# Low halves of ten weight slices: from VectorE to GpSimd

## The chip, the core and the metric

The kernel runs on one core of a Trainium2 chip. The metric is the device time of one execution in microseconds (us). Engines have short names here as in the profile: PE is TensorE (PEld its weight loads), DVE is VectorE, ACT is ScalarE, POOL is GpSimd, SP is SyncE, which issues most DMAs.

## What is computed

Three layers follow one another. The first is gated linear attention over 4 batches and 8 heads, 768 steps of 48 values: a state that decays by `alpha`, takes up `k` times `v`, and is read by `q`. Its output, 3072 tokens of 384 values, goes through a mixture of four experts, and that through a feed-forward layer with a clipped gate:

```
state = alpha[:, :, t, :, None] * state + einsum('bhd,bhe->bhde', k[:, :, t], v[:, :, t])
y[:, :, t] = einsum('bhd,bhde->bhe', q[:, :, t], state)
...
h = np.maximum(x @ w1[e], 0.0); out += p[:, e:e + 1] * (h @ w2[e])      # e = 0..3, 1024 hidden values each
...
h = x @ w_in; g = h * np.clip(h + 3.0, 0.0, 6.0) / 6.0; return g @ w_out   # 2048 hidden values
```

## The kernel before

**Three products for one.** Every matmul of the two layers runs on operands that are rounded to a shorter format. To keep the precision, a weight or an activation is split into a high half (rounded copy) and a low half (what the rounding lost), and three products are summed: high times high, low times high, high times low. A weight slice is 256 hidden values wide; its first matrix (y = 0) and its second (y = 1) each fill a tile of 128 partitions by 768 columns. So "slice i" has four tiles: `w0h`, `w0l`, `w1h`, `w1l`.

**Two phases.** In the first phase, the first some 490 us, the attention is computed, and between its steps PE works on the first seven weight slices (0 to 6: four of expert 0, three of expert 1) for the blocks of tokens as they become ready. The seven slices are split once, at the phase's start, and stay. The rest of the experts and the last layer are the second phase.

**The order is written out.** In the first phase a table of tokens (`PLAN`, then `BLOCK` for each later pair of blocks) sets the order in which the instructions of PE, DVE, ACT and SP are issued; each engine takes its own in order. Some tokens: `m0.6` is the first product of step 6 of visit 0 (line 923, `ph`), where steps 6 and 7 use slice 3; `o0.6` its second product (line 969, `po`); `a0.6` the high half of the result on ACT (line 933, `hh`); `h0.6` its low half on DVE (line 937, `hl`), which also sets the PSUM tile `ph` free for a step further on (two such tiles take turns). Visit 0 is expert 0 (slices 0 to 3), visit 1 expert 1 (slices 4 to 6: `m1.0` to `m1.5`). `r03` and `r13` round the weights of slice 3 on ACT (line 875, first and second matrix), and `l03` and `l13` compute their low halves (line 877). A token of the form `1.Uq3` is a step of the attention: `U` scales `kt` or `qt` in place (line 513), `M` masks the products `pa` (line 538), `S` copies on ACT (line 504).

**Rooms.** The raw weights lie in a few rooms (`rw`, `early_h`, `early_l`). When the low half of a slice is done, its room takes the next raw slice: `room_left` issues that load on SP (lines 859 and 864), which waits for the low half, and everything behind it on SP waits too.

**GpSimd** has no work between its constants at the start and the first weight combinations for the second phase.

The function that the change touches, as it stands before:

Of the kernel before, what the change touches and what calls it, by code (L numbers as in the profile page):

```python
# [11 lines left out]
F32 = mybir.dt.float32  # L12
# [708 lines left out]
def tile_gla__then__moe__then__moe2(  # L721
# [29 lines left out]
    nc = tc.nc  # L751
# [12 lines left out]
    mul, add, sub = ALU.mult, ALU.add, ALU.subtract  # L764
# [104 lines left out]
    def split_w(y, i):  # L869
        round_w(y, i)()  # L870

    def round_w(y, i):
        raw = raws.pop((y, i))
        hi, lo = (wpa.tile([P, 3 * SL], F32R, tag=f"w{y}{z}", name=f"w{y}{z}_{i}") for z in "hl")
        nc.scalar.copy(hi, raw)
        wts[(y, i)] = [t.rearrange("p (j f) -> p j f", j=KT if y == 0 else 2) for t in (hi, lo)]
        return lambda: nc.vector.tensor_tensor(lo, raw, hi.bitcast(F32), op=sub)


    xs = {}  # L880
# [158 lines left out]
    def do(tok, b):  # L1039
# [18 lines left out]
        elif kind == "g":  # L1058
            load_p(int(arg))
        elif kind in "Wrl":  # L1060
            y, i = int(arg[0]), int(arg[1])
            if kind == "W":
                if (y, i) == (1, 3):
                    again(0)
                load_w(y, i)
            elif kind == "r":
                splits[(y, i)] = round_w(y, i)
            else:
                splits.pop((y, i))()
                if (y, i) != (0, 1):  # L1070
                    room_left(y, i)
        else:
            vi, f = (int(x) for x in arg.split("."))
            vi += 2 * b
            if kind == "m":
                splits[(vi, f)] = mm1(vi, f)
            elif kind == "a":
                plan.pop((vi, f))()
            elif kind == "h":
                splits.pop((vi, f))()  # L1080
            elif kind == "o":
                mm2(vi, f)
                if f == len(visits[vi]["steps"]) - 1:
                    after(3, lambda v_=vi + 2: load_p(v_))
            else:
                finish(vi, f)
# [793 lines left out]
    for G in range(NG):  # L1880
        add_group(G)
        i = I_[G]
# [42 lines left out]
```

## Time and profile before

| | us |
|---|---|
| median of three runs | 1330.15 (1329.89 to 1330.52) |
| profiled execution, its own time | 1329.23 |
| its span, first to last instruction | 1327.5 |
| PE busy | 1305.6 (98%) |
| DVE busy | 893.3 (67%) |
| ACT busy | 586.4 (44%) |
| POOL busy | 130.4 (10%) |

The shares are means over stages that differ. DVE is busy for 67% of the span, but in the stage in which the ten low halves lie it is another matter, so the stage has to be read by itself. PE's clock has two levels here, 2.4 GHz (printed as 1.00) and 1.2 GHz (0.50); a number between is a stretch with both.

### The profile page before, as it was taken

What the parts mean: (1) busy time and instruction counts of PE and PEld (TensorE: products, weight loads), DVE (VectorE), ACT (ScalarE), POOL (GpSimd) and SP (SyncE); (2) the same over time, 40 slices, a digit from 0 to 9 for tenths busy, and PEclk for the clock granted to TensorE, in tenths of its full rate; (3) what the DMA queues carried; (4) which work ended last, traced back from release to release, by engine and by line L of the source; (5) the groups of instructions that cost most, each with busy time, mean ns of one, the idle gap of its engine ahead of it and who ended that gap; (6) DMA issues with size and microseconds to landing.
All of it is one profiled execution on the core that took longest, in us unless ns stands there. A gap on an engine that the chain in (4) does not pass through costs nothing.

```text
span 1327.5 us, 26799 instructions
## 1 busy us (share of the span) xinstructions
PE 1305.6 (98%) x10877; PEld 1088.3 (82%) x10877; DVE 893.3 (67%) x1635; ACT 586.4 (44%) x1065; POOL 130.4 (10%) x184
## 2 busy tenths in 40 slices
PE   8899999999999999999999999999999999999998
PEld 7799887888888888888888887888888888888886
DVE  8899977777875354778575557655887674445444
ACT  4655454444454232454442243234556554444442
POOL 4000000000000010323131102021321000000000
PEclk8899999999999999999999999999999999999999
DMA  7765536526342344899999969897965674436323
GB/s 207 208 170 132 163 108 167 148 72 186 108 128 70 116 143 158 252 307 308 352 273 298 253 205 281 250 287 229 265 196 204 233 210 148 148 137 175 127 87 48
DMA packets 164779, 250.75 MB, mean 189 GB/s; under 512 B 73520, under 2 KB 122544, under 8 KB 158128
## 3 DMA queue, kind: packets, MB, share of 16 engines
q1 hardware_dynamic: 145696, 222.90, 51.3%
q0 software_dynamic: 12480, 25.17, 11.4%
q10 hardware_dynamic: 6480, 0.98, 0.5%
q8 instruction: 85, 1.39, 0.4%
q14 instruction: 38, 0.31, 0.1%
HBM read 162.97 MB, written 90.75 MB: 191 GB/s over the span
## 4 chain that ended last, share of the span: by engine, by line
PE 88%; DVE 3%; ACT 3%; issue 2%; DMA 2%; POOL 1%; SPq 0%; ACTq 0%; DVEq 0%; POOLq 0%
PE sum L1637 29%; PE chain_b L1550 15%; PE ph L923 13%; PE chain_a L1550 12%; PE po L969 10%; PE po L1825 2%; PE py L628 2%; PE pa L525 2%; PE py L650 1%; PE pu L573 1%; DMA acc_d<-o 1%; DMA w_d<-da 1%; PE py L611 1%; ACT qt L481 1%; DVE kt L513 1%
## 5 line engine op out<-in xcount | busy, mean ns | idle before, releaser
L1637 PE MATMUL sum<-hh,V 128*128 128x512 f32 x1224 | 376.8, 389 | 0.4 <-DVE o L1687 0.4
L1637 PEld LDWEIGHTS sum<-hh,V 128*128 128x128 f32 x1224 | 229.7, 188 | 48.5 <-DVE o L1687 0.8
L1637 PE MATMUL sum<-hl,V 128*128 128x512 f32 x612 | 238.1, 389 | 0.0
L1570 DVE TENSOR_TENSOR cs<-ct,chain_b 128x512 f32<-128x512 f32 x153 | 105.0, 686 | 148.3 <-PE chain_b L1550 147.0
L1562 ACT COPY ct<-chain_a 128x512 f32<-128x512 f32 x153 | 89.2, 583 | 137.7 <-PE chain_a L1550 137.5
L1637 PEld LDWEIGHTS sum<-hl,V 128*128 128x128 f32 x612 | 114.9, 188 | 23.9
L933 ACT ACTIVATE hh<-ph 128x512 fp32r<-128x512 f32 (+1 forms) x98 | 52.4, 537 | 177.0 <-PE ph L923 175.7
L1587 ACT ACTIVATE hh<-cs 128x512 fp32r<-128x512 f32 x81 | 51.3, 633 | 137.9 <-DVE cs L1570 88.6
L937 DVE SCALAR_TENSOR_TENSOR hl<-ph,hh 128x512 fp32r<-128x512 f32 (+1 forms) x98 | 59.8, 612 | 71.4 <-ACT hh L933 71.3
L1596 ACT ACTIVATE g<-cs,three 128x512 f32<-128x512 f32 x72 | 52.2, 725 | 106.1 <-DVE cs L1570 104.2
L969 PE MATMUL po<-hh,w1h 128*128 128x512 f32 (+1 forms) x249 | 90.7, 372 | 0.0
L969 PE MATMUL po<-hh,w1l 128*128 128x512 f32 (+1 forms) x249 | 86.8, 356 | 0.0
L1601 DVE SCALAR_TENSOR_TENSOR hl<-g,hh 128x512 fp32r<-128x512 f32 x96 | 67.5, 705 | 27.2 <-ACT hh L1598 27.0
L969 PE MATMUL po<-hl,w1h 128*128 128x512 f32 (+1 forms) x249 | 80.7, 355 | 3.2 <-DVE hl L937 3.2
L923 PE MATMUL ph<-xh,w0h 128*128 128x512 f32 (+1 forms) x294 | 77.9, 374 | 2.0 <-DVE hl L937 1.1
L1597 DVE SCALAR_TENSOR_TENSOR g<-g,cs 128x512 f32<-128x512 f32 x72 | 50.4, 701 | 39.2 <-ACT g L1596 39.1
L1590 DVE SCALAR_TENSOR_TENSOR hl<-cs,hh 128x512 fp32r<-128x512 f32 x81 | 57.4, 710 | 28.7 <-ACT hh L1587 28.4
L923 PE MATMUL ph<-xl,w0h 128*128 128x512 f32 (+1 forms) x294 | 74.7, 363 | 0.0
L923 PE MATMUL ph<-xh,w0l 128*128 128x512 f32 (+1 forms) x294 | 74.6, 363 | 0.0
L1598 ACT ACTIVATE hh<-g 128x512 fp32r<-128x512 f32 x96 | 60.2, 630 | 20.9 <-DVE g L1597 18.8
L1688 POOL DMA_DIRECT2D acc_d<-o x54 | 47.9, 903 | 137.3 <-DVE o L1687 135.5
L923 PEld LDWEIGHTS ph<-xh,w0h 128*128 128x128 f32 x294 | 50.5, 191 | 12.2 <-DVE hl L937 3.1
(313 smaller groups left out, 2532.3 us busy)
## 6 DMA issues: line engine op xcount, KB each, us to landing
V<-ws_d SPq DMA_DIRECT2D x34, 1280.0 KB
V<-ws_d SPq DMA_DIRECT2D x34, 768.0 KB
ws_d<-V SPq DMA_DIRECT2D x17, 1280.0 KB
acc_d<-o POOLq DMA_DIRECT2D x54, 256.0 KB, 9.3
ws_d<-V SPq DMA_DIRECT2D x17, 768.0 KB
vl<-vd SPq DMA_DIRECT2D x96, 96.0 KB
draw<-in_moe_w_in_dram SPq DMA_DIRECT2D x8, 768.0 KB
w_d<-da SPq DMA_DIRECT2D x16, 384.0 KB
```

The lines of the kernel that those rows point to most:

```text
L923: pe.matmul(ph[:, 0:n], w[:, j, fs], x[:, j, cs], start=(o == 0 and j == 0), stop=(o == 2 and j == KT - 1),)
L933: high = lambda: nc.scalar.activation(hh[:, 0:n], ph[:, 0:n], AF.Relu)
L937: nc.vector.scalar_tensor_tensor(hl[:, 0:n], ph[:, 0:n], 0.0, hh[:, 0:n].bitcast(F32), op0=ALU.max, op1=sub)
L969: pe.matmul(accs[vi][m][:, 0:n], w[:, z, ms], h[:, 0:n], **fl)
L1550: pe.matmul(chain[bank], a, b, start=first_ and o == 0, stop=o == 2, skip_group_check=True)
L1562: o = act(512, lambda: nc.scalar.copy(CR.place(k), chain[0]), dep, d)
L1570: o = dve(512, lambda: nc.vector.tensor_tensor(SR.place(k), CR[kc], chain[1], op=add), dep, oc, d)
L1590: lambda: nc.vector.scalar_tensor_tensor(HR[k][1], get(), 0.0, HR[k][0].bitcast(F32), op0=ALU.max, op1=sub),
L1596: a = act(600, lambda: nc.scalar.activation(GR.place(kg), get(), AF.Relu, bias=three), dep, dg, opened)
L1598: hh = act(512, lambda: nc.scalar.activation(HR.place(k)[0], GR[kg], AF.Copy, scale=1.0 / 6.0), b, d)
L1601: lambda: nc.vector.scalar_tensor_tensor(HR[k][1], GR[kg], 1.0 / 6.0, HR[k][0].bitcast(F32), op0=mul, op1=sub),
L1637: pe.matmul(bank[(y, m)][:, ts], a, b[:, ts], start=first_ and x == 0, stop=last_ and x == 2, skip_group_check=True)
```

## The change

The low halves of slices 0 and 1 stay on DVE. Those of slices 2 to 6, ten instructions of 128x768, are issued on GpSimd:

```
         nc.scalar.copy(hi, raw)
         wts[(y, i)] = [t.rearrange("p (j f) -> p j f", j=KT if y == 0 else 2) for t in (hi, lo)]
-        return lambda: nc.vector.tensor_tensor(lo, raw, hi.bitcast(F32), op=sub)
+        low = nc.vector if i < 2 else nc.gpsimd
+        return lambda: low.tensor_tensor(lo, raw, hi.bitcast(F32), op=sub)
```

The order of PE, ACT and SP is the same before and after; DVE has ten rows fewer and POOL ten rows more. From here on, line numbers of the changed kernel are higher by one.

On DVE, at the first two low halves that move (slice 2; `w0l`, `w1l`), the order was this (`w` and `rq`, `dg` and `rq`, `kt` and `qt` are attention steps, `hl` is the low half of a result of step 1 and then of steps 2 and 3):

```order
L937 SCALAR_TENSOR_TENSOR hl_0_762<-ph_1_833,hh_0_761 128x256
L877 TENSOR_TENSOR w0l_846<-early_l,w0h_845 128x768
L877 TENSOR_TENSOR w1l_851<-early_l,w1h_850 128x768
L287 TENSOR_TENSOR w_2_914<-rq_704,rk_705 128x768
L513 TENSOR_TENSOR qt_790<-qt_790,tl_1_809 128x128x4
L345 TENSOR_REDUCE dg_917<-w_2_914 128x16
```

and now it is this; the two low halves are gone and `w` follows `hl` at once:

```order
L938 SCALAR_TENSOR_TENSOR hl_0_762<-ph_1_833,hh_0_761 128x256
L287 TENSOR_TENSOR w_2_914<-rq_704,rk_705 128x768
L513 TENSOR_TENSOR qt_790<-qt_790,tl_1_809 128x128x4
L345 TENSOR_REDUCE dg_917<-w_2_914 128x16
L290 TENSOR_TENSOR rq_704<-rq_704,ra_706 128x768
L513 TENSOR_TENSOR kt_769<-kt_769,tl_1_811 128x64x8
```

On POOL all ten stand behind the last constant (`mask`), in the order of the table, with slice 3's second matrix (`w1l_973`) ahead of its first (`w0l_1032`), and ahead of the first weight combination of the second phase (`spare_l`):

```order
L174 AFFINE_SELECT mask<-mask 64x64 x8
L878 TENSOR_TENSOR w0l_846<-early_l,w0h_845 128x768
L878 TENSOR_TENSOR w1l_851<-early_l,w1h_850 128x768
L878 TENSOR_TENSOR w1l_973<-early_h,w1h_972 128x768
L878 TENSOR_TENSOR w0l_1032<-rw_3_717,w0h_1031 128x768
L878 TENSOR_TENSOR w0l_1066<-early_h,w0h_1065 128x768
L878 TENSOR_TENSOR w1l_1069<-early_l,w1h_1068 128x768
L878 TENSOR_TENSOR w0l_1314<-early_l,w0h_1313 128x768
L878 TENSOR_TENSOR w1l_1498<-early_h,w1h_1497 128x768
L878 TENSOR_TENSOR w0l_1564<-early_h,w0h_1563 128x768
L878 TENSOR_TENSOR w1l_1595<-early_l,w1h_1594 128x768
L1478 TENSOR_TENSOR spare_l<-spare_h 128x256
```

Where DVE had `w1l_973` behind seven attention steps, POOL takes it as soon as its high half is there.

## Rows read from the trace of the kernel before

**Rows 1.** Windows: us, then PE, PEld, DVE, ACT, POOL busy, clock, DMA, GB/s.

```profile
50.00:100.00 50.00, 48.92 (x894) 45.36 (x893) 48.99 (x96) 28.13 (x54) 0.00 (x0) 0.93 0.68 189
```

**Rows 2.** Chain that ended last, 85 to 98 us: start us, length us, what.

```profile
90.77 0.34 DVE hl L937
...
91.16 1.34 PE ph L923 x9
...
97.59 0.34 DVE hl L937
...
97.97 0.39 PE ph L923
```

**Rows 3.** Waits of PE, 92 to 490 us: total us, times, longest.

```profile
PE ph L923 <- DVE hl L937: 0.7, 2, 0.3
```

**Rows 4.** Timeline of DVE, slice 2's low halves: start us, length us, instruction.

```profile
50.28 0.95 DVE L877 TENSOR_TENSOR w0l<-early_l,w0h 128x768 fp32r<-128x768 f32 x1
51.15 0.95 DVE L877 TENSOR_TENSOR w1l<-early_l,w1h 128x768 fp32r<-128x768 f32 x1
```

**Rows 5.** Timeline of POOL and DVE, where DVE reads PSUM (`po`).

```profile
465.42 0.46 POOL L1478 TENSOR_TENSOR spare_l<-spare_l,spare_h 128x128 f32<-128x128 f32 x1
465.84 0.74 POOL L1480 TENSOR_TENSOR spare_l<-spare_h 128x256 f32<-128x256 f32 x1
...
465.43 1.28 DVE L1836 TENSOR_TENSOR ft<-po,pb 128x512 f32<-128x512 f32 x2
```

**Rows 6.** Timeline of POOL and DVE, where DVE has two SBUF inputs.

```profile
528.57 0.75 POOL L1480 TENSOR_TENSOR wr<-wr 128x256 f32<-128x256 f32 x1
...
528.74 1.12 DVE L1590 SCALAR_TENSOR_TENSOR hl<-cs,hh 128x512 fp32r<-128x512 f32 x1
...
560.06 2.08 POOL L1477 TENSOR_TENSOR wr<-wr 128x256 f32<-128x256 f32 x1 [6.89 <-DMA wr<-in_moe_w_dram]
...
560.52 0.69 DVE L1590 SCALAR_TENSOR_TENSOR hl<-cs,hh 128x512 fp32r<-128x512 f32 x1
561.13 0.42 DVE L1409 TENSOR_TENSOR X18l<-pu,X18h 128x256 fp32r<-128x256 f32 x1
```

**Rows 7.** Timeline of ACT, DVE and PE around slice 3's low halves.

```profile
59.51 0.82 ACT L875 CAST w1h<-early_h 128x768 fp32r<-128x768 f32 x1
...
60.88 0.69 DVE L513 TENSOR_TENSOR qt<-qt,tl 128x512 f32<-128x512 f32 x1 [0.52 <-ACT kq L504]
61.49 0.42 DVE L937 SCALAR_TENSOR_TENSOR hl<-ph,hh 128x256 fp32r<-128x256 f32 x1
61.83 0.95 DVE L877 TENSOR_TENSOR w0l<-rw,w0h 128x768 fp32r<-128x768 f32 x1
62.69 0.68 DVE L538 TENSOR_TENSOR asb<-pa,mask 128x512 f32<-128x512 f32 x1
63.29 0.68 DVE L513 TENSOR_TENSOR kt<-kt,tl 128x512 f32<-128x512 f32 x1
...
62.83 0.62 PE L923 MATMUL ph<-xh,w0l 128*128 128x256 f32 x3
```

**Rows 8.** Timeline, windows (PE busy, clock) and chain of PE, 46 to 60 us.

```profile
49.49 0.62 PE L969 MATMUL po<-hl,w1h 128*128 128x256 f32 x3 [3.21 <-DVE hl L937]
...
51.00:52.00 1.00, 0.76 (x28) 0.50 1.05 217
...
52.37 4.14 PE ph L923 x18
...
58.12 2.15 PE ph L923 x18
```

**Rows 9.** Timeline of SP: DMA issues behind slice 2's and at slice 5's loads.

```profile
53.11 1.05 SPq L859 DMA_DIRECT2D early_l<-in_moe_w_dram  x2
...
61.40 2.78 SPq L246 DMA_DIRECT2D vl<-vd  x4
68.30 0.40 SPq L864 DMA_DIRECT2D early_h<-in_moe_w_dram  x1
```

## The prediction

> **What bounds the kernel now.** I read the windows first. From 50 to 100 us, where all ten low halves lie, PE is busy for 48.92 us and DVE for 48.99 of 50 [rows 1]. This is not the stage of the mean, where DVE has a third of its time free: here two engines run side by side, both full. The chain of waits says which of them sets the end. It runs mostly through PE, but at 91.16 and 97.97 us it comes from a DVE `hl`, and the product follows within 0.05 us of DVE's step [rows 2]. So DVE has no slack there: what DVE loses up to 98 us, PE loses. What DVE gains, PE can hardly use: from 92 to 490 us PE waits for `hl` for 0.7 us in all [rows 3]. A loss stays until the end, since behind it PE runs in a written order with almost no gaps in which to catch up.
>
> **What is removed.** Ten DVE instructions. Each holds DVE for 0.87 us, the distance of two that follow each other (51.15 less 50.28) [rows 4]; ten are 8.7 us.
>
> **What is added: GpSimd's time.** No GpSimd instruction of 768 columns is in the trace. With DVE out of the way, 128 columns take 0.46 us and 256 take 0.74 [rows 5], so 0.0022 us per column; 768 columns are 0.74 + 512 x 0.0022 = 1.86 us. The other bound is three times 0.74, 2.22 us; I take 1.86, as the fixed part is paid once. GpSimd is idle in this stage, so its time would be free if it were only its own.
>
> **What is added: DVE's waits.** It is not. Where a GpSimd instruction with two SBUF inputs meets a DVE one with two, one waits for the other: a DVE `hl<-cs,hh` of 128x512 that takes 0.69 us elsewhere takes 1.12 under a GpSimd instruction that began 0.17 us earlier, and a GpSimd instruction of 0.74 us takes 2.08 while three DVE instructions in a row (two shown) keep their usual 0.42 and 0.69 [rows 6]. Whoever runs first finishes, and DVE instructions on each other's heels keep GpSimd out. Where DVE reads PSUM, neither is longer: two of 128x512 take 1.28 us beside GpSimd's usual 0.74 [rows 5].
>
> Most DVE work from 50 to 93 us has two SBUF inputs (`kt`, `qt`, `w`, `rq`, `y`). So a low half on GpSimd will begin when DVE comes to an instruction on PSUM or to a reduction, run beside that, and then stop DVE until it ends. The cover is 0.34 us where it is an `hl` (61.49 to 61.83) and 0.60 where it is a mask step (62.69 to 63.29) [rows 7]. I take 0.60, as some begin beside two such steps. DVE then loses 1.86 - 0.60 = 1.26 us for each low half and saves 0.87: 0.39 net, 3.9 us for ten. One bound is no lock at all, -8.7 us on DVE; the other is no cover, 10 x (1.86 - 0.87) = 9.9 us.
>
> The Trainium skill says the same as a rule (SBUF — State Buffer, section Who interferes with whom): a DVE instruction with two SBUF inputs contends with a GpSimd instruction that reads SBUF, the later one blocks fully, and a DVE instruction with at most one SBUF input does not contend. This trace agrees with both halves (1.12 against 0.69; 1.28 and 0.74 undisturbed). Without the second half of the rule the sum would be 9.9 us, with it 3.9.
>
> **Who waits for a late low half.** For eight of ten there are microseconds between the low half and its first product. The tight ones are the first matrices of slices 3 and 6. Slice 3's ended on DVE at 62.78 us and PE used it at 62.83 [rows 7]. On GpSimd the second matrix of slice 3 stands ahead of it in the queue. That one's high half is ready at 60.33, so it runs to 62.2 at best, and stops DVE's `qt` of 60.88 [rows 7] meanwhile. Alone, the next would end 1.86 later at 64.05: 1.2 us late for PE. But DVE has been kept from `qt` and, if it arrives late from slice 2's lows, from the `kt` in front of it as well, 0.61 us each; then comes `hl` on PSUM, beside which GpSimd begins at some 63.4. The low half ends at 65.3, 2.4 us late. The `hl` that frees the tile `ph` for this product comes by 63.8, so the weights come last. These 2.4 us are not added to the 3.9: they are an early part of the same delay. DVE, kept back ten times, is 3.9 us late at 97.97, where PE has no slack; PE is then late by the larger of the two.
>
> **Queues.** SP's loads of slices 4 and 5 now wait for GpSimd. Two were issued by 54.2 us [rows 9]; slice 2's two low halves on GpSimd end near 52 and 55, so the second is some 1 to 2 us later, and behind it stand the loads of `vt` and `vl`. SP ended the last of these at 64.2 and then had nothing until 68.30 [rows 9]: 4.1 us of cover, so this costs nothing; without that gap it would cost up to 2 us. The load at 68.30 waited for slice 3's second low half, which GpSimd finishes at 62.2, so it is earlier. On POOL itself nothing stands behind the ten until 464 us, and all are done by then.
>
> **Sum.** The profiled execution took 1329.23 us, span 1327.5 and 1.7 around it. 1329.23 + 3.9 = 1333.1 by its own time; the median of the runs is 0.92 higher, 1330.15, and 1330.15 + 3.9 = 1334.05. I take 1334.0.
>
> **Rivals.**
>
> *The clock falls.* After an idle stretch of 3.21 us the granted clock was 0.50 (1.2 GHz) from about 51 us on, and 18 products took 4.14 us where the same 18 took 2.15 a little later [rows 8]. If PE stands idle for 2.4 us near 63 us, the same may follow: at least 2.0 us. PE is then 2.4 + 2.0 = 4.4 us late, and while it is slow DVE catches up, so the two are not added; with another fall further on, or the products around these 18, 6 us. 1330.15 + 5.2 (the middle) = 1335.3. Against it: the idle stretch is shorter and PE is full on both sides of it.
>
> *Not slower: the low halves slip in.* If GpSimd finds the port free at the right places (two PSUM steps or a reduction in a row), the cover is 0.99 us or more and DVE breaks even: 1.86 - 0.99 = 0.87. PE then gives 1.2 us at slice 3 and gets back up to 0.7 at the `hl` waits [rows 3]: +0.5, 1330.65. If the stop at slice 3 is covered too, -0.7, 1329.45. It decides at a mean stop of DVE of 0.87 us per low half. For it: `hl`, mask steps and reductions are frequent. Against it: DVE is full, and most of its rows have two SBUF inputs.
>
> *No cover.* The two engines take turns and each low half costs DVE its 1.86 whole: 9.9 us, 1340.05. For it: in rows 6 DVE got in between two GpSimd instructions and each waited for the other. Against it: GpSimd's low halves mostly come one at a time, as their high halves do.
>
> **How the numbers follow.** The forecast has 0.42, the clock 0.24, the low halves that slip in 0.24, no cover 0.10. The range has to leave out two in ten at most: it leaves out no cover and the better part of the gain, 1330.3 to 1337.0. About 0.2%, 2.66 us, is what a measurement of this kernel can tell from no change; from 1330.15 that is 1332.8. Of the forecast (3.9, spread some 2 to 5) 0.08 falls below that; so slower is 0.34 + 0.24 + 0.10 = 0.68. Faster by that much would need PE to gain 2.66 us where its waits for DVE give 0.7: 0.03. The rest, 0.29, is the same.
>
> **What would show it.** In the changed kernel's trace: low halves on POOL of 1.9 us or more, some well over; DVE rows with two SBUF inputs that are stretched by up to 1.9 us under them, and none on PSUM; the first product with slice 3's `w0l` two to three us behind its high products, waiting for POOL; the `ph` of 97.97 us some 4 us later, and the same shift at 490 us. I am wrong if DVE's rows keep their lengths, if the granted clock falls near 65 us, or if the shift at 98 us is made good before 490.

## The result, and the profile after

The changed kernel takes 1336.92 us in the median of 6 runs (1335.53 to 1338.54) against 1330.20 for the kernel before on the same chips (6 runs): a ratio of 1.0054, 95% interval 1.0038 to 1.0071, or 5 to 9.4 us. It is slower, as forecast, but by some 7 us where the forecast was 3.9. Taken from the 1330.15 us that the forecast starts from, the ratio gives 1337.3 us, just above the range.

The profiled execution took 1338.35 us, with a span of 1336.6, 9.1 more than before. Not all of that is the change: the first moved low half starts at 52.87 us, and the start-up before it is 2.8 us longer in this execution. So every shift below is taken from the `hl` at which both kernels still agree, the one at 49.02 us before and 51.81 after. Timeline of DVE in the kernel before (start us, length us, instruction): that `hl`, and the one of 97.49 us at which the shift was forecast.

```profile
49.02 0.42 DVE L937 SCALAR_TENSOR_TENSOR hl<-ph,hh 128x256 fp32r<-128x256 f32 x1
...
97.49 0.43 DVE L937 SCALAR_TENSOR_TENSOR hl<-ph,hh 128x256 fp32r<-128x256 f32 x1
```

The same view of the kernel after, with the rows between that changed:

```profile
51.81 0.42 DVE L938 SCALAR_TENSOR_TENSOR hl<-ph,hh 128x256 fp32r<-128x256 f32 x1
...
53.08 2.44 DVE L287 TENSOR_TENSOR w<-rq,rk 128x768 f32<-128x768 f32 x1
55.44 2.31 DVE L513 TENSOR_TENSOR qt<-qt,tl 128x512 f32<-128x512 f32 x1
...
63.86 2.02 DVE L513 TENSOR_TENSOR kt<-kt,tl 128x512 f32<-128x512 f32 x1
65.81 2.29 DVE L513 TENSOR_TENSOR qt<-qt,tl 128x512 f32<-128x512 f32 x1
68.02 0.41 DVE L938 SCALAR_TENSOR_TENSOR hl<-ph,hh 128x256 fp32r<-128x256 f32 x1
...
72.28 0.42 DVE L938 SCALAR_TENSOR_TENSOR hl<-ph,hh 128x256 fp32r<-128x256 f32 x1
73.70 0.42 DVE L538 TENSOR_TENSOR scratch1h<-pa,mask 128x256 f32<-128x256 f32 x1 [1.00 <-PE pa L525]
...
95.65 2.00 DVE L513 TENSOR_TENSOR kt<-kt,tl 128x512 f32<-128x512 f32 x1
97.57 2.17 DVE L294 TENSOR_TENSOR w<-rq,rk 128x384 f32<-128x384 f32 x1
99.66 0.41 DVE L938 SCALAR_TENSOR_TENSOR hl<-ph,hh 128x256 fp32r<-128x256 f32 x1
...
101.42 0.69 DVE L513 TENSOR_TENSOR qt<-qt,tl 128x512 f32<-128x512 f32 x1 [0.74 <-ACT qc L504]
...
106.43 0.42 DVE L938 SCALAR_TENSOR_TENSOR hl<-ph,hh 128x256 fp32r<-128x256 f32 x1
```

The last `hl` is 6.15 us late: (106.43 - 51.81) - (97.49 - 49.02). At the `hl` of 109.65 us of before the same difference is 7.00, and at 490 us it is 6.80. So the loss is made before 120 us and stays.

And POOL, the same view; these are what stretched the DVE rows:

```profile
52.87 1.83 POOL L878 TENSOR_TENSOR w0l<-early_l,w0h 128x768 fp32r<-128x768 f32 x1 [36.98 <-DMA ra<-in_alpha_dram]
54.64 2.56 POOL L878 TENSOR_TENSOR w1l<-early_l,w1h 128x768 fp32r<-128x768 f32 x1
63.50 1.84 POOL L878 TENSOR_TENSOR w1l<-early_h,w1h 128x768 fp32r<-128x768 f32 x1 [6.30 <-ACT w1h L875]
65.29 2.26 POOL L878 TENSOR_TENSOR w0l<-rw,w0h 128x768 fp32r<-128x768 f32 x1
72.23 1.83 POOL L878 TENSOR_TENSOR w0l<-early_h,w0h 128x768 fp32r<-128x768 f32 x1 [4.68 <-ACT w0h L875]
...
97.21 2.12 POOL L878 TENSOR_TENSOR w1l<-early_l,w1h 128x768 fp32r<-128x768 f32 x1
```

Read the two together. A low half that meets nobody takes 1.83 us. `w`, begun 0.21 us after the first, waits until it has ended and then does its usual work, 0.95 us; POOL's second low half, next in turn, waits for `w` (2.56 less 1.83 is 0.73), and then DVE's `qt` waits for that one. The `hl` of 72.28, which reads PSUM, runs under POOL's low half of 72.23 and keeps its 0.42 us. This picture repeats through the stage: nine low halves stop nine DVE rows, all with two SBUF inputs, for 13.45 us together (1.31 to 1.62 each, mean 1.49). The tenth, at 72.23, runs beside an `hl` and the 1.00 us before 73.70 in which DVE waits for PE, and stops nothing.

Timeline of PE after: the two waits that the stage gained.

```profile
68.58 0.59 PE L924 MATMUL ph<-xh,w0h 128*128 128x256 f32 x3 [3.05 <-DVE hl L938]
...
100.13 0.62 PE L924 MATMUL ph<-xh,w0h 128*128 128x256 f32 x3 [1.83 <-DVE hl L938]
```

The chain that ended last, after (start us, length us, what), answers to [rows 2]; it now leads through the stretched rows themselves:

```profile
65.88 2.21 DVE qt L513
68.10 0.34 DVE hl L938
68.44 0.14 issue
68.58 1.30 PE ph L924 x9
...
97.65 2.09 DVE w L294
99.74 0.34 DVE hl L938
```

Windows of the kernel after (us, then length and PE busy, PEld, DVE, ACT, POOL busy, granted clock, DMA, GB/s); the first answers to [rows 1], the second runs between two PE instructions, from the product behind the first `hl` above (`po<-hl`) to the first `pk` behind the last:

```profile
50.00:100.00 50.00, 42.25 (x738) 39.10 (x738) 47.76 (x75) 27.04 (x51) 20.16 (x10) 0.90 0.59 171
...
52.28:109.26 56.98, 51.38 (x880) 47.56 (x881) 54.76 (x87) 28.71 (x55) 20.16 (x10) 0.88 0.58 166
```

The stretch between the same two instructions of before:

```profile
49.49:99.24 49.75, 48.67 (x881) 45.15 (x881) 48.74 (x95) 28.64 (x55) 0.00 (x0) 0.93 0.69 191
```

PE does the same matmuls in both and takes 7.23 us longer for them: its idle time rose from 1.08 to 5.60 us, by 4.52, and its busy time by 2.71 at a lower mean clock. DVE reads as nearly full in both, but a DVE row that waits for the port counts as busy: 13.45 of its 54.76 us are waiting.

### The profile page after: what moved, and what is told of

It reads as the page before. It is cut to its first block, busy times and chain, and to the rows that moved or that the text cites. A ratio compares the mean times of both kernels' runs of the same rounds, so it can differ in the third digit from the quotient of the medians.

```text
span 1336.6 us, 26807 instructions
## 1 busy us (share of the span) xinstructions
PE 1307.3 (98%) x10877; PEld 1090.3 (82%) x10877; DVE 900.9 (67%) x1625; ACT 587.0 (44%) x1065; POOL 149.6 (11%) x194
## 4 chain that ended last, share of the span: by engine, by line
PE 87%; DVE 5%; DMA 3%; issue 2%; ACT 1%; SPq 1%; POOL 0%; DVEq 0%; POOLq 0%; ACTq 0%
PE sum L1638 29%; PE chain_b L1551 15%; PE chain_a L1551 12%; PE ph L924 12%; PE po L970 10%; PE po L1826 2%; PE py L628 2%; PE pa L525 1%; PE py L650 1%; DMA acc_d<-o 1%; PE pu L573 1%; DVE kt L513 1%; DMA ra<-in_alpha_dram 1%; PE py L611 1%; DMA w_d<-da 1%
```

## The experiments

Most kernels are the changed one with another rule for who computes the low halves (`i` is the slice): line 877, `low = nc.vector if i < 2 else nc.gpsimd`. The table gives how late the `hl` stand that were at 61.49, 66.63, 90.68 and 97.49 us before (`h0.4`, `h0.5`, `h1.3`, `h1.5` of the plan), and the `hl` near 490 us, each against the `hl` of 49.02; and the timed ratio to before with its interval. Profiled shifts come from one execution, ratios from the timed runs. The shifts have some play: in s4_alone and e9_only_5 the `hl` of 61.49 is 0.61 us early, although nothing ahead of it was changed (DVE's 0.52 us of waiting for ACT in [rows 7] is missing there), and between 113 and 490 us the shift of e7_slice_1 grows by 1.24 us, where nothing was changed either.

| kernel | GpSimd computes | 61.49 | 66.63 | 90.68 | 97.49 | 490 | ratio |
|---|---|---|---|---|---|---|---|
| changed | 2 to 6 | 3.74 | 2.86 | 6.19 | 6.15 | 6.80 | 1.0054 (1.0038 to 1.0071) |
| e1_write_only | fills only | -0.69 | -0.89 | -0.78 | -0.81 | -1.03 | 1.0006 (0.9996 to 1.0017) |
| e5_dve_twice | none, DVE twice | 1.37 | 2.36 | 8.31 | 9.30 | 9.02 | 1.0069 (1.0054 to 1.0084) |
| e2_keep_3_6 | 2, 4, 5 | 0.76 | 4.00 | 5.43 | 5.43 | 4.92 | 1.0041 (1.0026 to 1.0056) |
| e3_only_3_6 | 3, 6 | -0.61 | 0.23 | 4.94 | 4.90 | 6.43 | 1.0059 (1.0044 to 1.0074) |
| s2_alone | 2 | 0.77 | 0.75 | 0.78 | 0.78 | 1.12 | 0.9994 (0.9981 to 1.0006) |
| s3_alone | 3 | 1.12 | 0.94 | 0.60 | 0.61 | 0.60 | 1.0010 (0.9997 to 1.0023) |
| s4_alone | 4 | -0.61 | 2.64 | 2.92 | 2.93 | 2.46 | 1.0030 (1.0016 to 1.0043) |
| e9_only_5 | 5 | -0.62 | -0.61 | 0.05 | 0.05 | 0.29 | 1.0000 (0.9988 to 1.0012) |
| s6_alone | 6 | 0.11 | 0.11 | 2.19 | 2.15 | 2.20 | 1.0009 (0.9998 to 1.0021) |
| e7_slice_1 | 1 | 0.10 | 0.10 | 0.10 | 0.09 | 1.34 | 1.0005 (0.9990 to 1.0020) |
| e4_pieces | 2 to 6, in pieces | 0.13 | 0.84 | 4.05 | 5.43 | 6.14 | 1.0065 (1.0050 to 1.0080) |
| e6_h04_first | 2 to 6, `h0.4` earlier | 1.52 | 5.67 | 8.52 | 8.48 | 9.82 | 1.0071 (1.0049 to 1.0094) |

**Is it the port, or GpSimd being late?** From the kernel before: GpSimd is busy about as long after the rounding, but reads almost nothing: eight columns, then two fills.

```diff
-        return lambda: nc.vector.tensor_tensor(lo, raw, hi.bitcast(F32), op=sub)
+        def low_():
+            if i < 2:
+                return nc.vector.tensor_tensor(lo, raw, hi.bitcast(F32), op=sub)
+            nc.gpsimd.tensor_tensor(lo[:, 0:8], raw[:, 0:8], hi.bitcast(F32)[:, 0:8], op=sub)
+            for _ in range(2):
+                nc.gpsimd.memset(lo.bitcast(F32), 0.0)
+        return low_
```

> In place of each of the ten GpSimd subtractions: one of 8 columns (so that it still waits for the high half and holds the room) and then two fills of the low half with zero, 128x768, which write SBUF but read none. The low halves of slices 2 to 6 are left out of the result. By the rows of before a fill of 512 columns took 0.53 us, so GpSimd is busy for some 1.7 us per low half, as in the changed kernel. Port theory (GpSimd's reading of SBUF stops DVE): DVE rows under the fills keep their lengths, DVE is rid of 8.7 us, the first product with slice 3's low half waits for POOL by 1 to 2 us at most; in all 0.5 to 1.5 us below the kernel before, or up to 1 above it. Lateness theory (GpSimd's low halves come too late for their products): still 4 us or more above the kernel before.

The loss is gone: -0.81 us at 97.49, ratio 1.0006. Timelines of POOL, PE and DVE in this kernel:

```profile
62.57 1.53 POOL L882 MEMSET w0l<- 128x768 f32 x2
...
64.15 0.62 PE L929 MATMUL ph<-xh,w0l 128*128 128x256 f32 x3 [1.12 <-POOL w0l L882]
...
75.69 1.53 POOL L882 MEMSET w0l<- 128x768 f32 x2
...
76.36 0.54 DVE L370 TENSOR_TENSOR pr<-rv,dg 128x384 f32<-128x384 f32 x1
```

GpSimd was late here too: slice 3's first matrix made PE wait 1.12 us, and still nothing was lost in the end, since DVE, 8.7 us lighter and not stopped, had time in hand. The two fills keep 1.53 us beside DVE rows of every kind, and DVE rows with two SBUF inputs keep their lengths under them: `pr<-rv,dg`, begun under the fills of 75.69, takes 0.54 us, as everywhere. So it is GpSimd's reading that costs, not its lateness and not the queue. The Trainium skill says so (SBUF — State Buffer, section Who interferes with whom): a DVE instruction with two SBUF inputs contends with a GpSimd instruction that reads SBUF, not with one that only writes. This run agrees with that half too. The kernel shows a second thing: 8.7 us less work on DVE gave PE only 0.8 to 1.0 in the profiled execution, and nothing that the timed runs show.

**Does DVE's loss pass to PE one for one?** From the kernel before, with no GpSimd in it: DVE writes each moved low half twice.

```diff
-        return lambda: nc.vector.tensor_tensor(lo, raw, hi.bitcast(F32), op=sub)
+        def low_():
+            for _ in range(1 if i < 2 else 2):
+                nc.vector.tensor_tensor(lo, raw, hi.bitcast(F32), op=sub)
+        return low_
```

> The kernel before, with each of the ten low halves computed twice on DVE, one behind the other: 8.7 us more on DVE between 50 and 93 us and nothing on GpSimd. It prices DVE time in this stage. If DVE has no slack there: 8 us or more above before, about 1 us of PE time for 1 us of DVE time. If DVE has slack against PE, so that the change lost its time by other means: 4 us or less.

```profile
50.24 1.94 DVE L879 TENSOR_TENSOR w0l<-early_l,w0h 128x768 fp32r<-128x768 f32 x2
```

That pair lasts 1.94 us where one lasts 0.95, so a second writing adds 0.99 (it waits for the first); ten add 9.9, of which 9.30 arrive at the `hl` of 97.49, and the timed loss is 0.69%, 9.2 us. The step from DVE to PE stands, nearly one for one. PE's granted clock was 1.00 from 60 to 112 us here, so this is what DVE's time costs by itself.

**Which slices?** First the two with a tight first product apart from the rest.

```diff
-        low = nc.vector if i < 2 else nc.gpsimd
+        low = nc.gpsimd if i in (2, 4, 5) else nc.vector
```

> Slices 3 and 6, whose low halves are due at once, stay on DVE; 2, 4 and 5 are on GpSimd. Port theory: six stops of 1.49 us (the mean in the changed kernel) for six times 0.87 saved, +3.7 us on DVE, of which PE sees 3 to 4; less by 1.5 for each low half that falls into an idle stretch of DVE. Lateness theory: no loss, within 1 us of before, as the four that remain on DVE are the only ones that were due at once.

```diff
-        low = nc.vector if i < 2 else nc.gpsimd
+        low = nc.gpsimd if i in (3, 6) else nc.vector
```

> Only slices 3 and 6 on GpSimd, the rest on DVE. Port theory: four stops, 4 x (1.49 - 0.87) = +2.5 us, and some of the stall in front of slice 3's first product: 2 to 4 us above before, and together with the run that keeps 3 and 6 on DVE about the loss of the whole change. Lateness theory: the whole loss of the change, 6 to 7 us.

Both lose nearly as much as the whole change (5.43 and 4.90), more than the port theory had (3 to 4 and 2 to 4), so neither set carries it, and the two don't add up to it. The lateness theory had no loss for the first: as the cause of the whole it is out. In e3_only_3_6 PE's first wait was the predicted one, for slice 3's first low half; timeline of PE:

```profile
65.10 0.62 PE L924 MATMUL ph<-xh,w0l 128*128 128x256 f32 x3 [2.67 <-POOL w0l L878]
```

Then each slice by itself: `i == 2`, `i == 3`, `i == 4`, `i == 5`, `i == 6` in place of the sets above.

> Only the two low halves of slice 2 on GpSimd. Both follow one another and stop two DVE rows in turn (1.49 and 1.62 us in the changed kernel) for 1.74 us saved: hl of steps 2 and 3 are 1.4 us late. Sum theory (what counts is stops less savings, over the whole stage): +1.4 us at 98 us, less the 0.5 us in which DVE waits for ACT behind it: 0.9 to 1.4. Stall theory (a loss counts where it delays an hl or a low half for which PE then stands still, and by the half clock that follows a long idle stretch): no stall of over 0.5 us, no fall of the clock, so 1 us or less.

> Only the two low halves of slice 3 on GpSimd. Sum theory: less than 1 us, since with 3 and 6 moved the stops on DVE in this place were 0.2 and 1.0 us for 1.74 saved. Stall theory: PE waits for POOL by some 2.7 us in front of slice 3's first low product, as with 3 and 6 moved; the granted clock falls to 0.50 for some 3 us behind that, another 1.6, part of it covered: +2 to +3.5 us.

> Only the two low halves of slice 4 on GpSimd. Both have microseconds until their products, so lateness costs nothing. Sum theory: two stops of 1.5 to 1.6 us less 1.74, +1.3 to +1.5. Stall theory: the two stops come one behind the other in front of the hl that sets free the PSUM tile of step 7 (as in the run that kept 3 and 6 on DVE: the pair of qp steps took 3.87 us there), PE stands still for 2 to 3 us, the clock falls: +3 to +5 us.

> Only the two low halves of slice 5 on GpSimd, where both are due 4 us or more after their high halves and PE does not stand still. Port theory: two stops of 1.5 to 1.6 us for twice 0.87 saved, +1.2 to +1.5 us on DVE, all of which PE sees at 91 us, where it waits for DVE; no fall of the clock. Lateness theory: 0. A loss of 2 us or more would mean that a stop costs more than its own length.

> Only the two low halves of slice 6 on GpSimd. Sum theory: two stops of 1.3 and 1.6 us less 1.74, +1.2. Stall theory: both stops stand in front of the hl of step 3 of visit 1, for which PE waits with no slack at all (0.43 us in the kernel before); PE stands still for 2 us or more, the clock falls: +2.5 to +4.5 us.

They spread from 0.05 (slice 5) to 2.93 us (slice 4), or from 0.66 to 3.54 if the 0.61 us by which both were early at the start are counted, though each moves two instructions of the same size off DVE and stops it in two places. The difference is where the stops stand. Slice 4, timelines of POOL, DVE and PE:

```profile
68.06 2.00 POOL L878 TENSOR_TENSOR w0l<-early_h,w0h 128x768 fp32r<-128x768 f32 x1 [52.35 <-ACT w0h L875]
...
68.28 3.87 DVE L313 TENSOR_TENSOR qp<-rq,t 128x192 f32<-128x192 f32 x2
...
72.54 1.01 PE L924 MATMUL ph<-xh,w0h 128*128 128x256 f32 x3 [2.93 <-DVE hl L938]
```

Both low halves hit one pair of `qp` steps, each of the two once: 3.87 us where the pair takes 0.62. The next DVE row is the `hl` that PE waits for. DVE's own low halves of slice 4 came behind that `hl`, so nothing was saved ahead of it: 3.25 us of stops, in an execution that was 0.61 us early before them, are the 2.64 us of the table. What was saved afterwards became idle time of DVE: 0.89 us of waiting for PE, whose clock had fallen to 0.50 behind the 2.93 us, then 0.41 and 0.57 for ACT.

Slice 6 is the same at a smaller scale. Timeline of DVE in s6_alone:

```profile
87.61 2.01 DVE L513 TENSOR_TENSOR kt<-kt,tl 128x512 f32<-128x512 f32 x1
89.54 2.16 DVE L294 TENSOR_TENSOR w<-rq,rk 128x384 f32<-128x384 f32 x1
...
93.38 0.69 DVE L513 TENSOR_TENSOR qt<-qt,tl 128x512 f32<-128x512 f32 x1 [0.74 <-ACT qc L504]
```

Two stops of 1.32 and 1.61 us stand ahead of the `hl` of 90.68, and one of the two savings: 2.93 less 0.87 is 2.06, the table has 2.19. The second saving comes behind it and is spent at 93.38, where DVE now waits for ACT. PE's clock was 1.00 behind its wait of 1.99 us, so the 2.5 to 4.5 us of the stall theory did not come, and yet the loss is twice the sum theory's (1.2).

With slice 5 both savings stand ahead of the next such `hl`. Timeline of DVE in e9_only_5:

```profile
77.42 1.86 DVE L878 TENSOR_TENSOR w1l<-early_l,w1h 128x768 fp32r<-128x768 f32 x1
...
84.24 2.03 DVE L387 TENSOR_TENSOR pr<-pr 128x384 f32<-128x384 f32 x1
```

The first stop is 0.91 us (1.86 for 0.95), the second 1.48 (2.03 for 0.55): 2.39 less 1.74 is 0.65 us, and it arrives: from -0.61 at 66.63 to 0.05 at 90.68. In between DVE was later, 0.92 us at the `hl` of 82.55, and PE with it (0.91 at the `po` of 85.63), but at 91.16, where PE had stood idle in the kernel before, it was 0.12 us late: PE makes good what it would have waited anyway. Slice 2: 1.48 and 1.62 less 1.74 is 1.36, of which 0.78 is left, as DVE's 0.52 us of waiting in [rows 7] is missing here too. Slice 3 lost 0.61 us: PE waited 0.89 us for `hl` and 0.66 for the low half, not the 2.7 expected. In the timed runs only slice 4 can be told from no change.

**A slice outside the full stage.** `i == 1`, whose low halves stand ahead of 50 us.

> Only the two low halves of slice 1 on GpSimd, all others on DVE as before. They lie at 41 to 43 us of the kernel before, and behind them DVE has 0.4 and 1.9 us of idle time, in which it waits for ACT. Port theory with DVE's load: DVE steps behind them are stopped as elsewhere, by 1 to 1.5 us, but the loss falls into DVE's idle time: within 0.5 us of before. If a GpSimd low half cost its stop wherever it stands: 1.2 us or more.

```profile
43.70 1.48 DVE L489 TENSOR_TENSOR tl<-scratch0h 128x256 f32<-128x256 f32 x1 [2.31 <-ACT scratch0h L459]
...
47.07 0.69 DVE L513 TENSOR_TENSOR kt<-kt,scratch0h 128x512 f32<-128x512 f32 x1 [0.86 <-ACT kc L504]
```

DVE (timeline of e7_slice_1) is stopped there as well, by 1.06 us (1.48 for 0.42), but the wait for ACT that follows shrinks from 1.94 us in the kernel before to 0.86: 0.10 us arrive at 61.49, and the ratio is 1.0005. The 1.34 us at 490 us arise only behind 113 us, where nothing was moved; the ratio does not confirm them. Where DVE has idle time behind a stop, the stop costs nothing.

**Shorter pieces.** Six GpSimd instructions of 128 columns for each low half, so that no DVE row would wait for 1.83 us.

```diff
-        return lambda: nc.vector.tensor_tensor(lo, raw, hi.bitcast(F32), op=sub)
+        def low_():
+            if i < 2:
+                return nc.vector.tensor_tensor(lo, raw, hi.bitcast(F32), op=sub)
+            for c in range(0, 3 * SL, P):
+                cs = slice(c, c + P)
+                nc.gpsimd.tensor_tensor(lo[:, cs], raw[:, cs], hi.bitcast(F32)[:, cs], op=sub)
+        return low_
```

> The changed kernel with each low half in six GpSimd instructions of 128 columns instead of one of 768. By the rows of before a piece takes 0.42 us from start to start, six 2.5. Port theory: DVE and GpSimd take turns piece by piece, a DVE row with two SBUF inputs is never stopped by more than some 0.4 us, but there are six pieces to stop for: up to 2.5 us of stops per low half, less what runs beside PSUM steps, and a low half that takes 4 to 6 us to finish, so slice 3's comes later still. The loss from the first hl to 490 us grows from 6.8 us to 8 to 14. If only the length of the single stop counted (0.4 in place of 1.5 us), it would shrink to 3 or less.

Timelines of POOL and PE in e4_pieces:

```profile
67.11 3.83 POOL L882 TENSOR_TENSOR w0l<-rw,w0h 128x128 fp32r<-128x128 f32 x6
...
68.06 0.38 PE L929 MATMUL ph<-xh,w0l 128*128 128x256 f32 x1 [1.34 <-POOL w0l L882]
```

A stop is now 0.3 to 0.4 us, and DVE loses less at first (0.84 against 2.86 at 66.63). But each piece waits in its turn, a low half takes 2.5 to 4.7 us, and PE waits for POOL instead: 1.34, 0.76 and 0.87 us in slice 3, 1.28 in slice 6. The sum is much the same, 5.43 us at 97.49 and 6.14 at 490, neither the 8 to 14 that I expected nor the 3 or less. The loss changed sides.

**The `hl` that PE waited for, earlier.** The changed kernel with one entry of the plan moved, so that `h0.4` does not stand behind the stopped `qt`.

```diff
-| ... o0.2 1.C2 1.C3 1.Uq3 h0.4 r03 l03 m0.6 ...
+| ... o0.2 1.C2 1.C3 h0.4 1.Uq3 r03 l03 m0.6 ...
```

> The changed kernel with one token moved: the low half h0.4 of a result, for which PE stood still for 3.05 us, ahead of the step 1.Uq3 instead of behind it on DVE. Work, engines and GpSimd are the same. Stall theory (PE's long idle stretch and the clock's fall behind it are an own part of the loss): PE waits for 1 to 2 us instead of 3.05, then for slice 3's low half, the granted clock stays at 1.00 near 70 us, and the loss to 490 us falls from 6.8 us to 4.5 to 5.5. DVE theory (only DVE's sum of stops and savings counts): 6 to 7 us as before, since DVE does the same work in the same time.

The first wait shrank from 3.05 us to 0.84 and 0.67, and the clock stayed at 1.00 there. Yet the profiled loss grew, to 9.82 us at 490; the timed ratio is higher too (1.0071 to 1.0054), but the two intervals overlap. Timelines of DVE and PE in e6_h04_first:

```profile
67.99 3.76 DVE L313 TENSOR_TENSOR kp<-rk,t 128x192 f32<-128x192 f32 x2
...
72.67 0.77 PE L924 MATMUL ph<-xh,w0h 128*128 128x256 f32 x3 [3.36 <-DVE hl L938]
```

With the first wait gone, both low halves of slice 4 stopped DVE ahead of an `hl`, as in s4_alone, where in the changed kernel the first stopped nothing and the second a row behind that `hl`, and PE waits 3.36 us for the next `hl`. Neither theory's numbers came: I had taken the stops as fixed and only PE's wait as movable.

## Why the prediction was right or wrong

**Direction and mechanism: right.** DVE rows with two SBUF inputs are stretched under GpSimd's low halves, and none on PSUM is; e1_write_only shows that the reads are the cause. A DVE loss passes to PE (e5_dve_twice: 9.3 of 9.9). It is not made good later (7.00, then 6.80).

**GpSimd's own time: right.** 1.83 us against 1.86.

**DVE's wait: too small.** I took a cover of 0.60 us per low half, which left 1.26. The nine stops have a mean of 1.49, so the cover is 0.34 in the mean, or 13.45 us in all where I had 12.6. The mean is one of two kinds. Five low halves began beside an `hl` or a mask step, as I had thought: 1.31 to 1.50 us of stop, a cover of 0.33 to 0.52. Four had waited for a DVE row themselves (those of over 2.1 us on POOL), and the next DVE row then waited for nearly all of them: 1.60 to 1.62 us, a cover of some 0.22. The turns that the rival without cover described are there; its price, 1.86, is not.

**The sum: the step that failed.** I added ten stops, took off ten savings, read the result at the end of the stage, and put the clock at nothing. With the measured sizes that sum gives 13.45 - 8.7 = 4.75 us; measured are 6.15 at 97.49 and 7.00 at 109.65. The order was missing from it. PE takes what DVE owes at each `hl` that it waits for, and makes good only what it would have stood idle anyway. GpSimd works as soon as ACT has rounded, and DVE did so later in its written order, so the stops come early and the savings late. What counts is the debt at the `hl` at which PE has no slack, here that of 90.68 us: 13.45 less nine savings (7.83) is 5.62. 0.52 us of DVE's idling of before, at the `qt` of [rows 7], is taken off, and 1.00 us of new idling at 73.70, where DVE waits for a PE at half clock, is added: 6.10, where the table has 6.19. The tenth saving lies behind that `hl` and turns into the 0.74 us of waiting at 101.42. This adds up one trace and is no test. That a saving behind such an `hl` does not come back is what s6_alone shows, without any fall of the clock behind the wait: two instructions fewer on DVE, stops that exceed the savings by 1.2 us, and 2.2 us lost. (In s4_alone the 2.64 us are there before the clock falls.)

**Who is late at slice 3: the wrong one in the changed kernel.** I expected PE to wait 2.4 us for the low half of slice 3. PE waited 3.05 us, but for the `hl` behind the `kt` and `qt` that were stopped; that the place came out as forecast is luck. In e3_only_3_6 and e4_pieces it was the low half. Which is last hangs on tenths of a microsecond in how the instructions meet.

**SP's queue at no cost: nothing speaks against it.** In the stage PE's waits after name `hl` and `pb`, and no DMA.

**The clock: it fell, and it is a part of the loss.** I gave it 0.24 as a rival and named a fall near 65 us as a sign of being wrong; it came some 2 us later, counted from the first `hl`. Windows of the changed kernel, one behind each of the two new waits (of 3.05 and 1.83 us):

```profile
70.00:71.00 1.00, 1.00 (x7) 1.00 (x7) 1.00 (x3) 0.00 (x0) 0.00 (x0) 0.51 0.14 49
...
101.00:102.00 1.00, 1.00 (x9) 0.78 (x12) 0.58 (x1) 1.00 (x3) 0.00 (x0) 0.50 0.45 89
```

PE ran at 1.2 GHz there for some 3.4 us each time; this is where the 2.71 us of additional busy time come from. Timelines of PE before (first two lines) and after, for the first fall:

```profile
62.37 0.62 PE L923 MATMUL ph<-xh,w0h 128*128 128x256 f32 x3
...
67.25 0.52 PE L923 MATMUL ph<-xh,w0h 128*128 128x256 f32 x3
...
74.73 0.52 PE L924 MATMUL ph<-xh,w0h 128*128 128x256 f32 x3
```

Against the first `hl` (2.79 us apart), PE is 3.42 us late at 68.58, right behind its wait, and 4.69 at 74.73. The rival had 4.4 for this place. Behind the second wait it is 6.18 us late at 100.13 and 7.23 at 109.26; the `ph` of 97.97, which I expected some 4 us later, is 7.33 later. DVE then waits for PE:

```profile
114.27 0.35 DVE L602 TENSOR_TENSOR sc<-sd,pu 128x192 f32<-128x192 f32 x1 [0.89 <-PE pu L573]
```

Between the `hl` of 102.15 and that of 109.65 the shift grows by 0.84 us in the changed kernel, by 0.82 in e3_only_3_6 and by 0.84 in e6_h04_first, the three kernels whose clock had fallen behind PE's wait near the end of the stage. In the ten others it moves by 0.02 us at most, s6_alone among them, whose PE had waited 1.99 us there, as in e3_only_3_6, and kept its clock at 1.00. So 0.84 of the 7.00 us at 109.65 are the price of the second fall. The first fall cost DVE the 1.00 us at 73.70, but the low half of 72.23 ran in it and stopped nothing; what is left of it is not settled. A kernel that keeps PE busy through these waits would tell; none was run.

**The singles' sum proves nothing.** Five slices alone add up to 6.52 us, the whole to 6.15, but the pairs don't: 2 with 4 and 5 give 5.43 for 3.76, and 3 with 6 give 4.90 for 2.76. Stops shift the later work, and decide what the next low half meets.

## What to carry to other kernels

Before work goes from a full DVE to GpSimd, look at what DVE does meanwhile: where its rows have two SBUF inputs, a GpSimd instruction that reads SBUF stops DVE for nearly its whole length, here 1.49 us to save 0.87. Where two engines are both full, don't sum the gains and losses at the end of the stage; go from one handover to the next and carry the debt that stands there, since the other engine takes a delay at once and returns only what it would have stood idle itself. Add what its clock costs behind a long wait, here 0.84 us for one fall. The same move lost nothing where DVE has idle time (slice 1), where it reads PSUM, and where GpSimd only writes.

## What was not expected of the hardware

- Where two low halves stand one behind the other, GpSimd and DVE take turns in the changed kernel: a low half, one DVE row with two SBUF inputs, the next low half, the next DVE row (2.44, 2.56, 2.31 us in a row from 53 us on), unlike 560 us of before [rows 6], where GpSimd waited through a row of DVE instructions.
- Smaller GpSimd instructions don't make the lock cheaper: six of 128 columns take 3.83 us where one of 768 takes 1.83 to 2.56.
- After 1.83 us of waiting PE's clock fell in the changed kernel, and after 1.99 us in e3_only_3_6; after 1.99 us at nearly the same place in s6_alone it stayed at 1.00.
